# The second batch's Fourier transform in a fused FFT, SoLU and maxout kernel: x loaded earlier, its items set to other places

## The chip, the cores and the metric

The kernel runs on one core of a Trainium2 chip. The metric is the device time of one execution in microseconds (us), the lower the better. The kernel before took 2872.8 us (median of three runs, 2868.82 to 2873.03).

## The reference

Three layers one after the other, on x of 8 batches x 3072 positions x 256 channels:

```
X = rfft(x, axis=1);  y = irfft(X * (filt_r + 1j * filt_i), n=3072)          # per batch and channel
h = y @ w_in                                    # 256 -> 1024
solu = h * softmax(h);  ln = (solu - mean) / sqrt(var + 1e-6) * g_ln
z = ln @ w_out                                  # 1024 -> 256
m = maximum(maximum(z @ w1, z @ w2), z @ w3)    # 256 -> 768
out = m @ w_out2                                # 768 -> 256, float32
```

## The kernel before, in words

Engines are named as in the profile: PE (TensorE), PEld (its weight load), DVE (VectorE), ACT (ScalarE), POOL (GpSimd), SP (SyncE, which only issues transfers). Each works through its own queue in order. A framework schedules: it takes the program in the order in which it is written, moves instructions of one engine past each other by times that it reckons itself, and puts in the waits. What stands in each queue is therefore fixed before the kernel runs.

**Precision.** Values are kept as two 16-bit halves, a high and a low one, so nearly every product is three matmuls (high x high, high x low, low x high), and every result that PE makes is read twice: ACT writes the high half, DVE or POOL the difference.

**The steady loop.** A batch is cut into 6 groups of 512 positions (NG = 6), 48 groups in all. A group's work on PE is a string of items, whose order is the string ORDER (L27; the first group has FIRST, L26): z (two halves, `z_item`, 48 matmuls), h (four of 128 positions, `h_item`, 12 matmuls each, always for the next group or the one after), m (six blocks of the maxout, `m_item`, 18 matmuls each, whose three results lie in three PSUM buffers until ACT L573 and DVE L575 have taken their maximum), o (two, `o_item`, 36 each) and d (`d_item`, the last step of the inverse FFT for the group after next). PSUM has six small buffers ("r") for all of these but h, which has one of its own. `s0` to `s4` in the string are places: what the planner at L838 to L895 has put there (`put(batch, group, place, function, ...)`) is run at this point.

**The FFT of the next batch** goes into these places. Its steps for batch b: `load_x` (six pieces of 512 KB, POOL L106, into the one buffer called "x"), `absmax` (DVE L111, one per piece), `x_spread` and `x_scale` (the largest value over all partitions, through one PE product called amps, then small DVE operations), `prep_a` (ACT L153 and DVE L154 split a piece into halves xh, xl), `do_a` (six items "a", 6 matmuls each, results to DRAM scr_a by SP L176), `load_b` (POOL L184, reads bin back from scr_a and needs all six written), `do_b` (eight items "b"; their products with the filter on DVE L219/L220 and POOL L227/L228, then `late`: two halves yhl, transposed by SP L264 into yt), `do_c` (eight items "c" on yt, results over SP L388/L395 to scr_z), `load_d` and d. For batches 2 to 7 these are spread over nearly two batches' groups. For batch 1 there are only the first batch's groups 0 to 4: b stands in groups 2 and 3, c from the end of group 2 to group 4.

**What differs for batch 1 before the change.** Its x is loaded when the last setup job of group 0 has been put in the program (L1148 to L1150). Its filter table ft is multiplied by a factor on ACT when it has come (`scale_f`, L211), and yhl is split by ACT L257 and POOL L258; for later batches the factor is in the split itself (ACT L260, DVE L261).

**Setup.** The first batch's FFT is done ahead of the loop in float32. Its last step turns zx (which lies in buffer "x") by PE L354 (`first_turn_z`). The weights are converted and scaled meanwhile; of w_out2 the last piece is fetched at L1084, and its float32 form is put into the buffer "x" as wst (L1085), when zx has been read, by the jobs that group 0 runs at its `x0` places (`last`, `colsum`, `scale`, `split`, L1090 to L1102). The second halves of the maxout weights wm are written by POOL L704 just ahead of group 0. The second batch's x takes buffer "x" after wst, the third batch's after the second's, when the last `prep_a` has read it.

## Time and profile before

| | |
|---|---|
| median of three runs | 2872.8 us |
| the profiled execution: its time, its span | 2866.93 us, 2865.1 us |
| PE busy | 2801.6 us, 98% of the span |
| DVE, ACT, POOL busy | 70%, 43%, 40% |
| granted TensorE clock, mean | 0.990 |
| DMA | 352.73 MB, 123 GB/s on the mean |

The table is read so: PE is busy for 98% of the span, and its clock is nearly always granted in full. What is not PE's work is 63.5 us of idle time, and some time at the lower clock. The profile's slices of the span put nearly all of it into the first seventh, before 425 us: the setup, and groups 0 to 4 of the first batch.

### The profile page before, as it was taken

To read this page: it belongs to the slowest core of one execution; us is meant where nothing else is said; L and a number is where in the kernel's file an instruction comes from. 1 tells how busy PE (TensorE), PEld (TensorE's weight loads), DVE (VectorE), ACT (ScalarE), POOL (GpSimd) and SP (SyncE) were. 2 spreads that over 40 slices of the span, in tenths; PEclk is the share of its full clock that TensorE was granted. 3 is DMA by queue.
4 is the path that set the end of the run, shared out by engine and by line. 5 is a ranking of instruction groups with operands and counts; after the bars stand their busy time and mean duration, and the time that the engine had idled before them with its cause. 6 is when DMAs were issued, how large, how long until landed. Compare 5 with 4: busy or idle time off the path is not lost.

```text
span 2865.1 us, 49331 instructions
## 1 busy us (share of the span) xinstructions
PE 2801.6 (98%) x18923; PEld 1567.6 (55%) x18924; DVE 2000.6 (70%) x4158; ACT 1237.0 (43%) x2024; POOL 1138.6 (40%) x1208
## 2 busy tenths in 40 slices
PE   8799989999999999999999999999999999999999
PEld 7544545555555555555555555555555555555555
DVE  6787658777776776777677777777777677666563
ACT  5644444444443444444453444444444344333332
POOL 5343543444334443344334433344442444323222
PEclk8899999999999999999999999999999999999999
DMA  8445885668456874578555875567844576422221
GB/s 252 104 111 158 143 171 156 115 138 142 110 148 120 142 130 107 155 133 138 106 133 137 145 126 116 152 119 137 140 110 107 118 152 104 101 56 61 58 47 28
DMA packets 718380, 352.73 MB, mean 123 GB/s; under 512 B 620544, under 2 KB 663936, under 8 KB 718144
## 3 DMA queue, kind: packets, MB, share of 16 engines
q1 hardware_dynamic: 689040, 242.57, 44.0%
q0 software_dynamic: 28960, 106.95, 14.5%
q8 instruction: 148, 2.42, 0.4%
q14 instruction: 88, 0.72, 0.1%
q10 hardware_dynamic: 144, 0.07, 0.0%
HBM read 126.13 MB, written 71.30 MB: 69 GB/s over the span
## 4 chain that ended last, share of the span: by engine, by line
PE 90%; DMA 3%; POOL 2%; DVE 2%; issue 2%; ACT 1%; SPq 0%; ACTq 0%; POOLq 0%; DVEq 0%
PE mps L567 12%; PE mps L569 12%; PE mps L568 12%; PE hps L461 6%; PE hps L462 6%; PE hps L463 5%; PE zps L547 5%; PE zps L550 5%; PE zps L548 5%; PE ops L596 4%; PE ops L595 4%; PE ops L594 4%; DMA ft<-in_filt_dram 1%; PE bps L242 1%; PE bps L243 1%
## 5 line engine op out<-in xcount | busy, mean ns | idle before, releaser
L508 POOL TENSOR_TENSOR ul<-u,uh 128x1024 f16<-128x1024 f32 x191 | 410.7, 2150 | 1097.8 <-ACT uh L507 942.7
L567 PE MATMUL mps<-z,wm 128*128 128x512 f16 x1728 | 654.9, 379 | 2.6 <-DVE z L537 1.9
L569 PE MATMUL mps<-z,wm 128*128 128x512 f16 x1728 | 654.7, 379 | 1.1 <-DVE z L537 1.1
L568 PE MATMUL mps<-z,wm 128*128 128x512 f16 x1728 | 654.9, 379 | 0.0
L575 DVE SCALAR_TENSOR_TENSOR am<-mps,am 128x512 f32<-128x512 f32 x576 | 395.1, 686 | 211.2 <-PE mps L569 129.0
L472 DVE TENSOR_REDUCE mx<-hps 128x1 f32<-128x1024 f32 (+1 forms) x194 | 234.6, 1209 | 225.8 <-PE hps L463 225.5
L478 ACT ACTIVATE u<-hps,mx,scl 128x1024 f32<-128x1024 f32 (+1 forms) x194 | 231.6, 1194 | 311.2 <-DVE mx L475 307.1
L578 ACT ACTIVATE h<-am 128x512 f16<-128x512 f32 x288 | 180.5, 627 | 406.6 <-DVE am L575 406.6
L579 POOL TENSOR_TENSOR h<-am,h 128x512 f16<-128x512 f32 x240 | 278.1, 1159 | 188.5 <-ACT h L578 185.7
L596 PE MATMUL ops<-wo,h 128*128 128x256 f16 x1152 | 314.8, 273 | 4.0 <-DVE h L579 4.0
L594 PE MATMUL ops<-wo,h 128*128 128x256 f16 x1152 | 314.8, 273 | 0.5 <-ACT o L600 0.4
L595 PE MATMUL ops<-wo,h 128*128 128x256 f16 x1152 | 314.7, 273 | 0.0
L461 PE MATMUL hps<-win,y 128*128 128x512 f16 x768 | 293.9, 383 | 8.7 <-ACT y L436 6.5
L462 PE MATMUL hps<-win,y 128*128 128x512 f16 x768 | 293.5, 382 | 0.0
L463 PE MATMUL hps<-win,y 128*128 128x512 f16 x768 | 292.8, 381 | 0.0
L547 PE MATMUL zps<-ln,wo 128*128 128x512 f16 x752 | 285.4, 380 | 0.5 <-ACT o L600 0.5
L548 PE MATMUL zps<-ln,wo 128*128 128x512 f16 x752 | 285.4, 380 | 0.0
L489 DVE SCALAR_TENSOR_TENSOR u<-hps,mx,u 128x1024 f32<-128x1024 f32 (+1 forms) x194 | 246.4, 1271 | 51.5 <-ACT u L478 48.8
L507 ACT ACTIVATE uh<-u 128x1024 f16<-128x1024 f32 x192 | 202.7, 1056 | 184.1 <-DVE u L489 180.3
L569 PEld LDWEIGHTS <-wm 128*128 128x128 f16 x1728 | 169.0, 98 | 205.0 <-issue 1.3
L568 PEld LDWEIGHTS <-wm 128*128 128x128 f16 x1728 | 169.0, 98 | 201.7 <-issue 4.3
L567 PEld LDWEIGHTS <-wm 128*128 128x128 f16 x1728 | 169.0, 98 | 198.4
(232 smaller groups left out, 4482.4 us busy)
## 6 DMA issues: line engine op xcount, KB each, us to landing
out_dram<-o SPq DMA_DIRECT2D x95, 256.0 KB, 2.3
ft<-in_filt_dram POOLq DMA_DIRECT2D x56, 384.0 KB, 5.5
xt<-in_x_dram POOLq DMA_DIRECT2D x42, 512.0 KB, 8.2
scr_a<-ao SPq DMA_DIRECT2D x42, 512.0 KB, 3.3
bin<-scr_a POOLq DMA_DIRECT2D x56, 384.0 KB, 6.2
scr_z<-zt SPq DMA_DIRECT2D x56, 384.0 KB, 3.0
din<-scr_z POOLq DMA_DIRECT2D x42, 512.0 KB, 5.0
bt<-in_dft_b_dram POOLq DMA_DIRECT2D x56, 144.0 KB, 3.0
```

Source lines behind the costliest of these rows:

```text
L461: PE.matmul(o, y[:, dc, 0, tk], win[:, 0, dc, w], start=(dc == 0), stop=False)
L462: PE.matmul(o, y[:, dc, 0, tk], win[:, 1, dc, w], start=False, stop=False)
L463: PE.matmul(o, y[:, dc, 1, tk], win[:, 0, dc, w], start=False, stop=(dc == 1))
L508: (V if (b, g, i) == (0, 0, 3) else G).tensor_tensor(ul, u, uh, op=ALU.subtract)
L547: PE.matmul(ps, wo1[:, 0, c, w], ln[:, 0, c], start=(c == 0), stop=False)
L548: PE.matmul(ps, wo1[:, 1, c, w], ln[:, 0, c], start=False, stop=False)
L567: PE.matmul(pss[k], wm[k][:, 0, dc, w], z[:, dc, 0], start=(dc == 0), stop=False)
L568: PE.matmul(pss[k], wm[k][:, 1, dc, w], z[:, dc, 0], start=False, stop=False)
L569: PE.matmul(pss[k], wm[k][:, 0, dc, w], z[:, dc, 1], start=False, stop=(dc == 1))
L594: PE.matmul(o, h2[:, j, 0, tk], wo2[:, 0, j], start=(j == 0), stop=False)
L595: PE.matmul(o, h2[:, j, 0, tk], wo2[:, 1, j], start=False, stop=False)
L596: PE.matmul(o, h2[:, j, 1, tk], wo2[:, 0, j], start=False, stop=(j == 5))
```

## The change

1. Two more places per group, `s5` behind x1 and `s6` behind m4.
2. The second batch's x is loaded right behind the first batch's last turn: the six `load_x(1, i)` stand ahead of `pads()`, and buffer "x" no longer holds wst. For this w_out2's float32 form is made in place, in the three buffers that its pieces were fetched into (`last` with the new `low`), and its column sums and its split go in three parts instead of two and one.
3. The second batch's `absmax`, `x_spread`, `x_scale` and first `prep_a` go to group 0, its six a items over group 1 (one each place instead of two), its b and c items into groups 2 and 3 alternately, the last c to the first place of group 4 instead of the second.
4. The third batch's x is loaded piece by piece in groups 1 to 3 instead of six pieces in a row; its loads, and its first two `prep_a` on ACT, keep the program's order in their queues.
5. `scale_f` is gone. The second batch's yhl is split as the later ones' are: ACT with the factor, and DVE in POOL's stead.

```
@@ -24,7 +24,7 @@
 
 
 FIRST = "h0 m0 x0 h1 m1 x0 x0 h2 m2 x0 x0 x0 s0 s1 s2 x2 h3 m3 d m4 m5 g0 f o0 s3 o2 g1 s4"
-ORDER = "z0 s0 z1 s1 h2 m0 x0 x0 x1 m1 x0 x0 m2 s2 x2 h3 m3 d m4 m5 g0 f o0 s3 o2 g1 s4"
+ORDER = "z0 s0 z1 s1 h2 m0 x0 x0 x1 s5 m1 x0 x0 m2 s2 x2 h3 m3 d m4 s6 m5 g0 f o0 s3 o2 g1 s4"
 
 
 @with_exitstack
@@ -103,7 +103,9 @@
             x_t[b] = one.tile([128, 6144], F32, tag="x", name="xt")
         src = x[b].rearrange("(p r) d -> p (r d)", r=24)
         c = slice(i * 1024, (i + 1) * 1024)
-        G.dma_start(out=x_t[b][:, c], in_=src[:, c])
+        ins = G.dma_start(out=x_t[b][:, c], in_=src[:, c])
+        if b == 2:
+            tc.keep_in_program_order(ins)
 
     def absmax(b, i):
         if i == 0:
@@ -150,7 +152,9 @@
         xh = two.tile([128, 1024], F16, tag="zo", name="xh")
         xl = two.tile([128, 1024], F16, tag="bin", name="xl")
         src = x_t[b][:, s * 1024:(s + 1) * 1024]
-        S.activation(xh, src, AF.Copy, scale=scl[b][:, 0:1])
+        ins = S.activation(xh, src, AF.Copy, scale=scl[b][:, 0:1])
+        if b == 2 and s < 2:
+            tc.keep_in_program_order(ins)
         V.scalar_tensor_tensor(xl, src, scl[b][:, 0:1], xh, op0=ALU.mult, op1=ALU.subtract)
         xhl[b, s] = (xh, xl)
 
@@ -206,9 +210,6 @@
         bt_t[0, u], ct_t[0, u] = t[:, 0:4], t[:, 4:8]
 
     yT_t, zt_t = {}, []
-
-    def scale_f(b, u):
-        S.activation(f_t[b, u], f_t[b, u], AF.Copy, scale=pf[:, 1:2])
 
     def products(pss, ft, u, outs=None):
         yfs = []
@@ -253,14 +254,10 @@
             for dc in range(2):
                 yv = yfs[dc].rearrange("p k r s -> p k (r s)")
                 yhl = yhl_t[2 * (u % 2) + dc]
-                if b < 2:
-                    S.activation(yhl[:, :, 0:48], yv, AF.Copy)
-                    G.tensor_tensor(yhl[:, :, 48:96], yv, yhl[:, :, 0:48], op=ALU.subtract)
-                else:
-                    S.activation(yhl[:, :, 0:48], yv, AF.Copy, scale=pf[:, 1:2])
-                    V.scalar_tensor_tensor(
-                        yhl[:, :, 48:96], yv, pf[:, 1:2], yhl[:, :, 0:48], op0=ALU.mult, op1=ALU.subtract
-                    )
+                S.activation(yhl[:, :, 0:48], yv, AF.Copy, scale=pf[:, 1:2])
+                V.scalar_tensor_tensor(
+                    yhl[:, :, 48:96], yv, pf[:, 1:2], yhl[:, :, 0:48], op0=ALU.mult, op1=ALU.subtract
+                )
                 SP.dma_start_transpose(out=yt[:, dc], in_=yhl.rearrange("p k s -> p (k s)"))
         return early, late
 
@@ -640,9 +637,12 @@
                     wprep(v, (raw[:, k:k + 1], True))
                 return
             S.activation(dst, raw.bitcast(F32).rearrange("p a (n w) -> p a n w", w=2)[:, :, :, 1], AF.Copy, scale=REBIAS)
-            lo = raw.rearrange("p a (n w) -> p a n w", w=2)[:, :, :, 0]
-            top = raw.bitcast(U16).rearrange("p a (n w) -> p a n w", w=4)[:, :, :, 1]
-            G.tensor_scalar(lo, top, TOP, 7.5 * 2.0 ** -8 - 0.5, op0=ALU.mult, op1=ALU.add)
+            low(raw)
+
+    def low(raw):
+        lo = raw.rearrange("p a (n w) -> p a n w", w=2)[:, :, :, 0]
+        top = raw.bitcast(U16).rearrange("p a (n w) -> p a n w", w=4)[:, :, :, 1]
+        G.tensor_scalar(lo, top, TOP, 7.5 * 2.0 ** -8 - 0.5, op0=ALU.mult, op1=ALU.add)
 
     def wconv(pairs):
 
@@ -668,7 +668,7 @@
         av = []
 
         def sizes():
-            for v, (pool, tag) in zip(parts, ((one, "o"), (two, second))):
+            for v, (pool, tag) in zip(parts, ((one, "o"), (two, second), (two, second))):
                 kn = v.shape[1]
                 ab = pool.tile([128, 1024], F16, tag=tag, name="wab").bitcast(BF16)[:, :kn * n]
                 av.append(ab.rearrange("p (k n) -> p k n", k=kn))
@@ -812,11 +812,7 @@
         held[0] = None
 
     def do_b(b, u):
-        if u == 0 and b == 1:
-            scale_f(b, 0)
         run(b_item(b, u))
-        if u < 7 and b == 1:
-            scale_f(b, u + 1)
         if u < 6:
             load_tabs(b, u + 2)
             load_b(b, u + 2)
@@ -836,7 +832,7 @@
         run(it)
 
     NT = NB * NG
-    slots = [[[] for _ in range(5)] for _ in range(NT)]
+    slots = [[[] for _ in range(7)] for _ in range(NT)]
 
     def put(b, c, s, f, *a):
         if b >= 0:
@@ -846,13 +842,13 @@
 
         if b == 1:
             for i in range(6):
-                put(0, i // 4, (3, 4, 0)[i // 2], absmax, 1, i)
-            put(0, 1, 0, x_spread, 1)
-            put(0, 1, 1, x_scale, 1)
-            put(0, 1, 1, prep_a, 1, 0)
-            put(0, 1, 1, prep_a, 1, 1)
+                put(0, 0, (1, 2, 3)[i // 2], absmax, 1, i)
+            put(0, 0, 3, x_spread, 1)
+            put(0, 0, 4, x_scale, 1)
+            put(0, 0, 4, prep_a, 1, 0)
+            put(0, 1, 0, prep_a, 1, 1)
             for s in range(6):
-                put(0, 1, 2 + s // 2, do_a, 1, s)
+                put(0, 1, (0, 1, 5, 2, 6, 3)[s], do_a, 1, s)
             for u in range(2):
                 put(0, 1, 2 * u, load_tabs, 1, u)
                 put(0, 1, 4, load_b, 1, u)
@@ -877,15 +873,15 @@
             put(b - 2, 5, 0, load_c, b, 0)
         if b + 1 < NB:
             at = (
-                ((0, 1, 3), (0, 1, 4), (0, 2, 0), (0, 2, 1), (0, 2, 2), (0, 2, 3)) if b == 1 else
+                ((0, 1, 4), (0, 2, 1), (0, 2, 3), (0, 3, 0), (0, 3, 5), (0, 3, 3)) if b == 1 else
                 [(b - 1, *s) for s in ((0, 0), (0, 2), (0, 4), (1, 1), (1, 3), (2, 0))]
             )
             for i in range(6):
                 put(*at[i], load_x, b + 1, i)
 
         if b == 1:
-            at = [(2, 1), (2, 2), (2, 3), (2, 4), (3, 1), (3, 2), (3, 3), (3, 4)]
-            ct = [(2, 3), (2, 4), (3, 1), (3, 2), (3, 3), (3, 4), (4, 0), (4, 1)]
+            at = [(2, 1), (2, 5), (2, 2), (2, 6), (2, 4), (3, 5), (3, 2), (3, 6)]
+            ct = [(2, 2), (2, 6), (2, 3), (3, 0), (3, 2), (3, 6), (3, 3), (4, 0)]
         else:
             at = [(u // 2, 2 * (u % 2)) for u in range(8)]
             ct = [((u + 1) // 2, (4, 1)[u % 2]) for u in range(8)]
@@ -1082,15 +1078,26 @@
     first_turn_z(4)
     first_turn_z(5)
     get(19)()
-    wo2_32 = wview(one.tile([128, 6144], F32, tag="x", name="wst"), 6, 256)
-    todo += blocks(w_out2, wo2_32)
+    for i in range(6):
+        load_x(1, i)
     pads()
     G.dma_start(out=dA, in_=dft_a[:, 0:2])
 
+    wo2_32 = []
+
     def last():
         for i in range(17, 20):
-            pre(i)()
-        conv(17, 18, 19)()
+            pair = got.pop(i)[0].rearrange("p a (n w) -> p a n w", w=2)
+            low(pair.rearrange("p a n w -> p a (n w)"))
+            wo2_32.append(pair[:, :, :, 1].bitcast(F32))
+            lo, hi = pair[:, :, :, 0], pair[:, :, :, 1]
+            V.scalar_tensor_tensor(lo, hi, -0x80000000, lo, op0=ALU.bitwise_and, op1=ALU.bitwise_or)
+            S.activation(wo2_32[-1], wo2_32[-1], AF.Copy, scale=REBIAS)
+            V.scalar_tensor_tensor(hi, hi, 3, lo, op0=ALU.logical_shift_left, op1=ALU.bitwise_or)
+
+    def split_o2():
+        for i, v in enumerate(wo2_32):
+            wsplit(wo2[:, :, 2 * i:2 * i + 2], v, pw["o2"], G)
 
     def set_kap():
         V.tensor_tensor(kap, pw["o1"][:, 0:1], pw["m"][:, 0:1], op=ALU.mult)
@@ -1098,8 +1105,8 @@
         V.tensor_scalar(kap, kap, 2.0 ** -14, None, op0=ALU.mult)
 
     jobs.append(last)
-    jobs += colsum([wo2_32[:, 0:4], wo2_32[:, 4:6]], 256, wmax, 12, "zo")
-    jobs += [scale("o2", 12, 1), split(wo2, wo2_32, "o2", G), set_kap]
+    jobs += colsum(wo2_32, 256, wmax, 12, "zo")
+    jobs += [scale("o2", 12, 1), split_o2, set_kap]
 
     for t in range(NT):
         b, c = divmod(t, NG)
@@ -1145,9 +1152,6 @@
             elif k == "x":
                 if i == 0:
                     fill(1)
-                    if not jobs and NB > 1 and 1 not in x_t and t == 0:
-                        for k in range(6):
-                            load_x(1, k)
                 if i == 1 and nx2 and nx2[1] == 0:
                     flush()
                     load_d(*nx2)
```

How the queues move, at three places on POOL and ACT. Line numbers behind "in the kernel after" are those of the changed file, in which L496 is what L499 was, L403 was L406, L505 was L508, L576 was L579, L188 was L184, L193 was L189, L475 was L478, L570 was L573, L504 was L507, L575 was L578; L257 is its `late`.

POOL just ahead of group 0 in the kernel before (din is a load for the first batch's d items, wm the maxout weights' low halves, st a small power):

```order
L645 TENSOR_SCALAR wraw<-wraw 128x512
L406 DMA din_2003<-scr_94 128x1024
L499 TENSOR_TENSOR st<-st,mhalf 128x4
L704 TENSOR_TENSOR wm_79<-w_880,wm_79 128x384
L704 TENSOR_TENSOR wm_79<-w_881,wm_79 128x384
L704 TENSOR_TENSOR wm_78<-wln,wm_78 128x2x384
```

and in the kernel after:

```order
L645 TENSOR_SCALAR wraw<-wraw 128x512
L403 DMA din_2033<-scr_94 128x1024
L496 TENSOR_TENSOR st<-st,mhalf 128x4
L106 DMA xt<-in_x_dram 128x1024
L704 TENSOR_TENSOR wm_79<-w_880,wm_79 128x384
L704 TENSOR_TENSOR wm_79<-w_881,wm_79 128x384
L106 DMA xt<-in_x_dram 128x1024
L704 TENSOR_TENSOR wm_78<-wln,wm_78 128x2x384
L106 DMA xt<-in_x_dram 128x1024
```

The second batch's first piece of x now stands ahead of the weights' low halves; the fourth to sixth follow between and behind their second halves, and none is left where all six stood, behind the split of w_out2 in group 0.

POOL around the first loads of bin, the second batch's way back from scr_a, in the kernel before (xt here is the third batch's x):

```order
L508 TENSOR_TENSOR ul<-u,uh 128x1024
L106 DMA xt<-in_x_dram 128x1024 x6
L184 DMA bin<-scr_a_93 96x8x256
L508 TENSOR_TENSOR ul<-u,uh 128x1024
L184 DMA bin<-scr_a_93 96x8x256
L189 DMA bt<-in_dft_b_dram 96x768
```

and in the kernel after:

```order
L106 DMA xt<-in_x_dram 128x1024
L496 TENSOR_TENSOR st<-st,mhalf 128x4
L581 TENSOR_SCALAR st<-st,kap 128x4
L576 TENSOR_TENSOR h_2164<-am,h_2164 128x512
L505 TENSOR_TENSOR ul<-u,uh 128x1024
L188 DMA bin<-scr_a_93 96x8x256 x2
L106 DMA xt<-in_x_dram 128x1024
L505 TENSOR_TENSOR ul<-u,uh 128x1024
L193 DMA bt<-in_dft_b_dram 96x768
```

Two pieces of the third x are now ahead of the bin loads, one right behind them, and three stand much later, in groups 2 and 3.

ACT in group 3, in the kernel before (u is an h item's exponential, am the first step of an m item's maximum, ft the filter table, uh the high half of u, h that of the maximum):

```order
L478 ACTIVATE u,st<-hps,mx,scl 128x1024
L573 ACTIVATE am<-mps 128x512
L211 ACTIVATE ft<-ft,pf 128x768
L507 ACTIVATE uh<-u 128x1024
L573 ACTIVATE am<-mps 128x512
L578 ACTIVATE h_3618<-am 128x512 x2
```

and in the kernel after:

```order
L475 ACTIVATE u,st<-hps,mx,scl 128x1024
L570 ACTIVATE am<-mps 128x512
L504 ACTIVATE uh<-u 128x1024
L575 ACTIVATE h_3661<-am 128x512
L570 ACTIVATE am<-mps 128x512
L257 ACTIVATE yhl_90<-p_3731,pf 128x8x48
L257 ACTIVATE yhl_91<-p_3737,pf 128x8x48
```

The filter's own pass no longer stands between the first and the second am; the split of yhl, with the factor pf, follows the second.

## Rows read from the trace of the kernel before

**Rows 1.** The page's first part: busy time, share, instructions of each engine.

```profile
PE 2801.6 (98%) x18923; PEld 1567.6 (55%) x18924; DVE 2000.6 (70%) x4158; ACT 1237.0 (43%) x2024; POOL 1138.6 (40%) x1208
```

**Rows 2.** Windows by stage: length, then busy by engine, clock, DMA share, GB/s.

```profile
138.90:198.08 59.18, 51.80 (x276) 27.72 (x274) 49.07 (x103) 31.98 (x50) 28.86 (x26) 0.97 0.52 119
...
259.75:327.31 67.56, 61.07 (x486) 34.57 (x485) 48.72 (x95) 26.09 (x44) 35.61 (x47) 0.95 0.69 161
327.31:403.03 75.72, 63.34 (x554) 36.86 (x551) 43.50 (x94) 29.76 (x52) 40.26 (x52) 0.93 0.97 166
403.03:423.53 20.50, 16.61 (x126) 8.62 (x126) 10.33 (x32) 7.99 (x15) 9.21 (x13) 0.92 1.09 231
423.53:2865.10 2441.57, 2437.24 (x16319) 1331.50 (x16317) 1703.13 (x3525) 1031.13 (x1684) 941.52 (x963) 1.00 0.58 117
```

**Rows 3.** Windows at the lower clock behind 138 us: the longest, all four summed.

```profile
360.40:370.60 10.20, 5.06 (x70) 3.46 (x70) 4.12 (x9) 5.50 (x9) 5.36 (x5) 0.50 1.11 171
...
sum 23.90, PE 16.71 PEld 10.41 DVE 12.49 ACT 8.10 POOL 12.06; mean PE 4.18 PEld 2.60 DVE 3.12 ACT 2.02 POOL 3.02
```

**Rows 4.** Waits of PE: us in total, times, the longest.

```profile
PE cps L377 <- ACT am L573: 8.4, 1, 8.4
PE bps L242 <- DMA bin<-scr_a: 6.5, 1, 6.5
PE ops L596 <- DVE h L579: 4.0, 1, 4.0
PE cps L377 <- DMA yt<-yhl: 3.9, 2, 3.2
```

**Rows 5.** Timeline of DVE: start, us, instruction, count, idle before and its releaser.

```profile
146.42 1.27 DVE L489 SCALAR_TENSOR_TENSOR u<-hps,mx,u 128x1024 f32<-128x1024 f32 x1
...
186.83 1.22 DVE L111 TENSOR_REDUCE xm<-xt 128x1 f32<-128x1024 f32 x1 [3.09 <-DMA xt<-in_x_dram]
187.97 0.68 DVE L579 TENSOR_TENSOR h<-am,h 128x512 f16<-128x512 f32 x1
...
208.86 0.29 DVE L129 TENSOR_REDUCE amr<-amps 128x1 f32<-128x128 f32 x1 [3.84 <-PE amps L127]
...
212.59 2.47 DVE L154 SCALAR_TENSOR_TENSOR xl<-xt,scl,xh 128x1024 f16<-128x1024 f32 x2
```

**Rows 6.** Timeline of POOL: x's loads, bin's first, the maxout weights' low halves.

```profile
134.53 1.79 POOL L704 TENSOR_TENSOR wm<-w,wm 128x384 f16<-128x384 f32 x2 [0.40 <-ACT wm L703]
137.33 1.75 POOL L704 TENSOR_TENSOR wm<-wln,wm 128x768 f16<-128x768 f32 x1 [1.01 <-ACT wm L703]
...
175.49 3.26 POOL L106 DMA_DIRECT2D xt<-in_x_dram  x6
...
254.97 3.24 POOL L106 DMA_DIRECT2D xt<-in_x_dram  x6 [3.18 <-DVE xl L154]
272.67 0.83 POOL L184 DMA_DIRECT2D bin<-scr_a  x1 [14.46 <-DMA scr_a<-ao]
```

**Rows 7.** Timeline of ACT: the filter's pass in group 3.

```profile
361.98 0.94 ACT L211 ACTIVATE ft<-ft,pf 128x768 f32<-128x768 f32 x1 [10.85 <-DMA ft<-in_filt_dram]
```

**Rows 8.** The chain, by time: start, us, what (a matmul's pace, the filter's way).

```profile
201.70 1.73 PE zps L550 x8
...
348.84 13.05 DMA ft<-in_filt_dram
```

**Rows 9.** Line L354, zx's turns: ns min/median/max, first and last start (us).

```profile
L354 PE MATMUL zps<-eye_f,zx x48: 272/273/421, 79.1 to 138.8; 128*128 128x128 f32 x48
```

**Rows 10.** Tile xt, all of the span: its loads.

```profile
DMA to landing us min/median/max: 4.1/8.2/13.8
```

**Rows 11.** Tile yt between 270 and 430 us: its transposes.

```profile
DMA to landing us min/median/max: 3.1/4.6/13.8
```

**Rows 12.** Line L261 from 425 to 2000 us: ns min/median/max; DVE's idle before it.

```profile
L261 DVE SCALAR_TENSOR_TENSOR yhl<-p,pf,yhl x72: 602/620/1102, 536.9 to 1975.3; 128x384 f16<-128x384 f32 x72
...
  ACT yhl L260: 82.0, 54
```

More of the change, by code (lines that the diff above doesn't have):

```diff
@@ L642, in wprep, with low @@
             S.activation(dst, raw.bitcast(F32).rearrange("p a (n w) -> p a n w", w=2)[:, :, :, 1], AF.Copy, scale=REBIAS)
-            lo = raw.rearrange("p a (n w) -> p a n w", w=2)[:, :, :, 0]
-            top = raw.bitcast(U16).rearrange("p a (n w) -> p a n w", w=4)[:, :, :, 1]
-            G.tensor_scalar(lo, top, TOP, 7.5 * 2.0 ** -8 - 0.5, op0=ALU.mult, op1=ALU.add)
+            low(raw)
+    def low(raw):
+        lo = raw.rearrange("p a (n w) -> p a n w", w=2)[:, :, :, 0]
+        top = raw.bitcast(U16).rearrange("p a (n w) -> p a n w", w=4)[:, :, :, 1]
+        G.tensor_scalar(lo, top, TOP, 7.5 * 2.0 ** -8 - 0.5, op0=ALU.mult, op1=ALU.add)
     def wconv(pairs):
@@ L670, in sizes @@
         def sizes():
-            for v, (pool, tag) in zip(parts, ((one, "o"), (two, second))):
+            for v, (pool, tag) in zip(parts, ((one, "o"), (two, second), (two, second))):
                 kn = v.shape[1]
@@ L838 @@
     NT = NB * NG
-    slots = [[[] for _ in range(5)] for _ in range(NT)]
+    slots = [[[] for _ in range(7)] for _ in range(NT)]
     def put(b, c, s, f, *a):
@@ L1084, with split_o2 @@
     get(19)()
-    wo2_32 = wview(one.tile([128, 6144], F32, tag="x", name="wst"), 6, 256)
-    todo += blocks(w_out2, wo2_32)
+    for i in range(6):
+        load_x(1, i)
     pads()
     G.dma_start(out=dA, in_=dft_a[:, 0:2])
+    wo2_32 = []
     def last():
         for i in range(17, 20):
-            pre(i)()
-        conv(17, 18, 19)()
+            pair = got.pop(i)[0].rearrange("p a (n w) -> p a n w", w=2)
+            low(pair.rearrange("p a n w -> p a (n w)"))
+            wo2_32.append(pair[:, :, :, 1].bitcast(F32))
+            lo, hi = pair[:, :, :, 0], pair[:, :, :, 1]
+            V.scalar_tensor_tensor(lo, hi, -0x80000000, lo, op0=ALU.bitwise_and, op1=ALU.bitwise_or)
+            S.activation(wo2_32[-1], wo2_32[-1], AF.Copy, scale=REBIAS)
+            V.scalar_tensor_tensor(hi, hi, 3, lo, op0=ALU.logical_shift_left, op1=ALU.bitwise_or)
+    def split_o2():
+        for i, v in enumerate(wo2_32):
+            wsplit(wo2[:, :, 2 * i:2 * i + 2], v, pw["o2"], G)
     def set_kap():
@@ L1100 @@
     jobs.append(last)
[L1101 to L1102 removed]
+    jobs += colsum(wo2_32, 256, wmax, 12, "zo")
+    jobs += [scale("o2", 12, 1), split_o2, set_kap]
     for t in range(NT):
@@ L1147 @@
                     fill(1)
-                    if not jobs and NB > 1 and 1 not in x_t and t == 0:
-                        for k in range(6):
-                            load_x(1, k)
                 if i == 1 and nx2 and nx2[1] == 0:
```

48 lines of the change are left out of this document (20 added, 28 removed).

## The prediction

> **What bounds the kernel now.** I read the busy line first: PE works for 2801.6 of 2865.1 us [rows 1], so only PE's waits, or time at the lower clock, can be won. The windows by stage say where these are [rows 2]. From 423.53 us to the end PE is busy for 2437.24 of 2441.57 us at a granted clock of 1.00. What each queue holds from the middle of group 4 on is the same in both kernels, so whatever is won or lost before that point is carried to the end one for one. In groups 0, 2, 3 and the start of group 4 PE idles for 7.38, 6.49, 12.38 and 3.89 us. (z0 of group 1 starts at 198.08, of group 2 at 259.75, of group 3 at 327.31, of group 4 at 403.03.)
>
> The list of PE's waits names what ended them [rows 4]: 4.0 us for h of DVE L579 (group 0), 6.5 for bin (group 2), 8.4 for an am of ACT L573 (group 3), 3.9 for yt (group 4). One step further back, on the timelines: h was late because the x maximum ahead of it on DVE stood 3.09 us for x's landing [rows 5]; bin was late because POOL issued it at 272.67, after scr_a had come back, behind the six pieces of the third x issued from 254.97 on [rows 6]; am was late because ACT stood 10.85 us in L211 for the filter [rows 7], whose way took 13.05 us [rows 8].
>
> The granted clock is the last view. Behind each of these waits stands a stretch at 0.50, the lower of the two levels (1.2 of 2.4 GHz): four windows of 23.90 us with 16.71 us of PE work [rows 3]. At full clock this work takes half, so 8.36 us are lost to it.
>
> **What the change takes away.** Group 0: the maxima of x stand early in the group instead of ahead of h: 4.0; the other 3.4 us of its idle time I leave where they are. Group 2: the bin wait, since only two single pieces of x stand ahead of bin and the a items end half a group sooner: 6.49. Group 3: L211 is gone, and what it held with it: 12.38. Group 4: yt is filled earlier, by b items that end in group 3: 3.89. Clock, if the waits ahead of it go: 8.36. Sum 35.1 us.
>
> **What the change adds.** For each: both ends, and the value I take.
>
> 1. POOL now stands at x's first piece until zx's last turn has read the buffer, 138.8 + 0.27 = 139.1 [rows 9]; in before POOL did the low halves of wm from 134.53 on [rows 6]. A load holds POOL for 3.26 / 6 = 0.54. So the last low half is ready at 139.1 + 0.54 + 1.79 + 0.54 + 1.75 = 143.7, 4.6 us later than before. PE begins at 138.90 with h0's 12 matmuls of 0.216 us (1.73 / 8, [rows 8]), to 141.5, and has m0's products of the high halves next. Ends 0 and 2.2; taken 0.5.
> 2. Three of the x maxima stand on DVE ahead of the first u (L489, at 146.42 in before, [rows 5]); behind it are the am that free m's PSUM, and h1 needs the buffer that u reads. The third piece is issued at 143.7. With the shortest way of x's loads, 4.1 us [rows 10], it is there at 147.8; maximum 1.22, u 1.27 and four small steps of some 0.2 bring u's end to 151.1. PE has m0 and m1 to do ahead of h1: 36 matmuls, 7.8 us, to 149.3. So 1.8 us are lost by the shortest way and 5.9 by the median, 8.2. The pieces are issued 2.3 us apart now and not in a row, so I lean to the shortest, and part of the loss falls into the 3.4 us of idle time that I left. Ends 0 and 5.9; taken 1.5.
> 3. The first a item, now at group 1's first place, needs the chain from amr (208.86) to the first xl (212.59 plus half of 2.47): 5.0 us [rows 5]. Ahead of it PE has z0, 24 matmuls, 5.2 us. Ends 0 and 2.5 (if another xl stands ahead); taken 0.6.
> 4. c0 stands behind 66 matmuls and a b item's start after b0, some 15 us, in which b0's products, its split and the transpose must pass; the transpose alone takes 3.1 to 13.8 us [rows 11]. Ends 0 and the 3.9 of the yt waits in before; taken 1.
> 5. Six maxima of the third x stand singly in groups 1 to 3, five of them soon behind their loads. Ends 0 and five times 3.09 [rows 5], 15.5; taken 2, since most loads have over half a group.
> 6. The 16 subtractions of yhl move from POOL to DVE, at 0.62 us each, and DVE waits for ACT's half ahead of them: 82.0 / 54 = 1.52 us a time in the later batches [rows 12]. In groups 2 and 3 DVE has 48.72 + 43.50 = 92.2 us of work beside PE's 61.07 + 63.34 = 124.4 [rows 2]. 16 x 0.62 makes it 102.1, and with 16 x 1.52 = 24.3 of waits 126.5: 2.1 above PE. Ends 0 and 24.3; taken 3, the 2.1 and a little for unevenness.
>
> At nothing I cost w_out2 in place: its parts go through as many passes on ACT and DVE as before (three of each kind), and in before its split was done when the x loads were issued behind it at 175.49 [rows 6], 12.5 us before DVE began the h that o waited for, at 187.97 [rows 5]. Only what overruns these 12.5 us would cost time.
>
> The costs add to 8.6 us and the net gain is 35.1 - 8.6 = 26.5. The profiled execution took 2866.93 us (span 2865.1), so it becomes 2840.4. It stands 5.9 below the median of three, 2872.8; against that median the forecast is 2846.3, and I put down 2846.
>
> For items 2 and 5 the way of a 512 KB load is the open figure, and the trace has 4.1, 8.2 and 13.8 us [rows 10]. The Trainium skill, "DMA: Bandwidth & Descriptors", section "Anatomy of one DMA — SWDGE (gpsimd) path", gives about 2.0 us and the bytes at 436 GB/s; by that an estimate is 3.2 us, and both items would cost under 1 us. No load of x in this trace was that quick, so the measured way decides.
>
> **The rivals.**
>
> A. DVE becomes the bound of groups 2 and 3. Items 5 and 6 then cost not 5 but some 20 of their 39.8 us (8 and 12). For it: 126.5 beside 124.4 us. Against it: DVE's other waits are for PE, and shrink when PE is not held up. The gain is 35.1 - 3.6 - 20 = 11.5: 2861.
>
> B. The moved subtractions are slow beside POOL. L261 has a median of 620 and a longest of 1102 ns [rows 12]: 16 x 0.48 = 7.7 us more on DVE, which in groups 2 and 3 has no room left. 2846 + 7.7 = 2854. Against it: the median of 72 is within 18 ns of the least. The Trainium skill, "SBUF — State Buffer", section "Who interferes with whom", has the rule for this: DVE and GpSimd share one pair of ports, and the one that comes second waits for the other's whole instruction. By that the subtraction, with both its inputs in SBUF, would stand behind POOL's passes; the trace's median says that this is rare.
>
> C. The filter and yt come late all the same. L219 on DVE reads the filter itself now, so the 13.05 us way [rows 8] can hold DVE where it held ACT. Then group 3's 12.38 and the clock behind it, 2.5 (half of 5.06, [rows 3]), stay: 2846 + 14.9 = 2861. For it: the DMA share in that stage is already 0.97 [rows 2]. Against: ACT passes all m items, DVE's queue reaches L219 only when PE has done the b item, which gives the filter longer.
>
> D. Slower. The eight maxima that stand close behind their loads (three of item 2, five of item 5) meet ways of 13.8 instead of 8.2 us: 8 x 5.6 = 45 us of DVE standing still, in which h, am and z stand too. From the point where all losses pass 35.1 us, it is slower; with 34 of the 45 reaching PE and the 5.1 of items 1, 3, 4 and 6 it is 2872.8 + 4 + 2 of lower clock behind the new waits: 2879. Against it: 13.8 is the longest of all loads, and single loads press the queues less than six in a row.
>
> E. The waits only change their names: each stage is then held by the next chain (b's way to c, say) at the same length. 2872. Against it: groups 2 and 3 each wait once and long, for one instruction.
>
> **How the numbers follow.** Forecast 0.64, its own range 2837 to 2854; A 0.15, B 0.07, C 0.08, D 0.04, E 0.02. The range of 8 in 10 reaches down to where nearly nothing of the added costs arrives (35.1 less 1: 2838.7, and 4 us for what of group 0's left idle time goes too: 2835), and up past A and C to 2863. About 0.2% (5.7 us) is what a measurement of this kernel can tell from no change. Faster than that are the forecast, B, and nearly all of A and C: 0.91; within 0.2% are E and a tail of A and C: 0.05; slower is D: 0.04.
>
> **What would show it.** Right: z0 of group 1 starts near 193 us, of group 2 near 255, of group 3 near 316, of group 4 near 378; no wait of DVE for x next to the h of o in group 0; no wait of PE for bin and none for am behind a filter; no window at half clock behind 150 us. New and small: PE's waits at m0 and h1 in group 0 (items 1 and 2), at the first a item, for yt at c0, DVE's waits for x in groups 1 to 3 and for yhl in groups 2 and 3; their sum on PE should be near 8.6. Wrong: DVE busy or waiting for the whole of groups 2 and 3 with PE waiting for z, h or am (A); L261's counterpart near 1 us (B); DVE waiting for ft (C); clock still 0.93 to 0.95 there, which would leave the 8.36 unwon.

## The result and the profile after

The kernel after takes 2840.2 us (median of 4) where the kernel before takes 2870.8 in the same runs: ratio of the means 0.9897, interval 0.9867 to 0.9927. A second measurement of the unchanged pair gave 2847.1 against 2862.2, ratio 0.9949, interval 0.9930 to 0.9969. Both are faster; 2846 was forecast, between 2835 and 2863. The profiled execution took 2841.28 us (span 2839.5), 25.6 less than that of before.

The busy line, as in [rows 1]:

```profile
PE 2795.4 (98%) x18923; PEld 1563.6 (55%) x18924; DVE 2015.1 (71%) x4174; ACT 1233.8 (43%) x2021; POOL 1125.8 (40%) x1194
```

Windows by stage, as in [rows 2] (length, then busy by engine, clock, DMA share, GB/s). The bounds are the starts of h0 of group 0 and of z0 of groups 1 to 5, and the end. First the kernel after:

```profile
138.53:193.69 55.16, 51.57 (x278) 27.67 (x276) 50.99 (x103) 35.34 (x57) 33.65 (x30) 0.97 0.52 131
193.69:255.35 61.66, 61.60 (x330) 32.37 (x328) 50.49 (x97) 32.43 (x50) 18.91 (x14) 1.00 0.45 120
255.35:320.80 65.45, 61.45 (x549) 35.45 (x548) 48.15 (x100) 25.86 (x44) 36.97 (x52) 1.00 0.95 182
320.80:383.81 63.01, 61.08 (x523) 35.50 (x519) 50.02 (x103) 27.55 (x48) 33.81 (x44) 0.97 1.05 200
383.81:440.75 56.94, 56.94 (x348) 30.63 (x347) 41.60 (x88) 25.95 (x42) 17.93 (x15) 1.00 0.55 132
440.75:2839.50 2398.75, 2394.36 (x16067) 1307.80 (x16065) 1670.72 (x3465) 1011.45 (x1652) 925.90 (x950) 1.00 0.57 117
```

and the last two stages of the kernel before, cut at the same items:

```profile
403.03:466.40 63.37, 59.48 (x378) 32.27 (x378) 42.63 (x92) 28.22 (x47) 24.80 (x26) 0.97 0.68 160
466.40:2865.10 2398.70, 2394.37 (x16067) 1307.85 (x16065) 1670.84 (x3465) 1010.91 (x1652) 925.92 (x950) 1.00 0.58 117
```

From z0 of group 5 on the two are alike to 0.05 us. So everything was won in the stretch from h0 of group 0 to z0 of group 5: 327.50 us before, 302.22 after, 25.28 less. Groups 0 and 1 together give 4.03 of it (120.85 to 116.82), groups 2 to 4 give 21.25. By the windows, 20.6 us of it are PE's idle time (30.1 to 9.6) and 4.7 are work that no longer runs at the lower clock. What PE waited for in the stretch, as in [rows 4] (us in total, times, the longest):

```profile
PE mps L565 <- DVE wm L707: 2.8, 1, 2.8
PE bps L243 <- ACT am L570: 2.1, 2, 1.8
PE cps L374 <- DVE y L434: 1.7, 1, 1.7
PE mps L564 <- ACT am L570: 1.2, 1, 1.2
PE ops L593 <- POOL h L576: 0.6, 1, 0.6
```

None of the four long waits is left. Two windows at the lower clock remain, one behind the first of these waits and one behind the third; [rows 3] had four of 23.90 us:

```profile
144.75:148.20 3.45, 3.45 (x9) 1.31 (x10) 3.45 (x6) 3.18 (x6) 3.43 (x4) 0.53 0.69 180
363.40:366.90 3.50, 3.44 (x52) 2.46 (x52) 3.24 (x8) 1.68 (x4) 3.33 (x5) 0.51 0.88 204
```

The 2.8 us are new. They end with DVE's pass on wm, which took 1.02 us in the kernel before, begun when the first two of POOL's passes of [rows 6] had ended (timeline of DVE: start, us, instruction, idle before):

```profile
136.55 1.02 DVE L707 SCALAR_TENSOR_TENSOR wm<-wln,pwm,wm 128x768 f16<-128x768 f32 x1 [3.56 <-ACT wm L706]
```

and 4.41 in the kernel after (DVE, then POOL):

```profile
140.28 4.41 DVE L707 SCALAR_TENSOR_TENSOR wm<-wln,pwm,wm 128x768 f16<-128x768 f32 x1 [2.79 <-ACT wm L706]
148.90 1.00 DVE L707 SCALAR_TENSOR_TENSOR wm<-wln,pwm,wm 128x768 f16<-128x768 f32 x1
```

```profile
139.00 0.60 POOL L106 DMA_DIRECT2D xt<-in_x_dram  x1 [4.64 <-PE zps L351]
139.62 1.79 POOL L704 TENSOR_TENSOR wm<-w,wm 128x384 f16<-128x384 f32 x2
141.35 0.56 POOL L106 DMA_DIRECT2D xt<-in_x_dram  x1
141.93 1.65 POOL L704 TENSOR_TENSOR wm<-wln,wm 128x768 f16<-128x768 f32 x1
143.51 0.57 POOL L106 DMA_DIRECT2D xt<-in_x_dram  x1
144.10 2.23 POOL L704 TENSOR_TENSOR wm<-w,wm 128x384 f16<-128x384 f32 x2
```

DVE's pass starts in the middle of POOL's passes on wm and ends 1.1 us behind the third of them, and the fourth and fifth take 2.23 instead of 1.79: each engine held up the other. Of DVE's and ACT's waits in the stretch these matter below:

```profile
DVE xm L113 <- DMA xt<-in_x_dram: 16.9, 5, 5.4
DVE yhl L258 <- ACT yhl L257: 12.2, 11, 2.6
```

```profile
ACT yhl L257 <- POOL p L229: 23.1, 14, 4.0
ACT yhl L257 <- POOL p L231: 7.0, 2, 6.3
```

### The profile page after: what moved, and what is told of

The parts are those of the page before. It is cut to its first block, busy times and chain, and to the rows that moved or that the text cites. A ratio compares the mean times of both kernels' runs of the same rounds, so it can differ in the third digit from the quotient of the medians.

```text
span 2839.5 us, 49318 instructions
## 1 busy us (share of the span) xinstructions
PE 2795.4 (98%) x18923; PEld 1563.6 (55%) x18924; DVE 2015.1 (71%) x4174; ACT 1233.8 (43%) x2021; POOL 1125.8 (40%) x1194
## 4 chain that ended last, share of the span: by engine, by line
PE 91%; DVE 3%; POOL 2%; issue 1%; DMA 1%; ACT 1%; SPq 0%; ACTq 0%; POOLq 0%; DVEq 0%
PE mps L564 12%; PE mps L566 12%; PE mps L565 12%; PE zps L544 6%; PE zps L545 6%; PE zps L547 6%; PE hps L458 5%; PE hps L459 5%; PE hps L460 5%; PE ops L593 4%; PE ops L592 4%; PE ops L591 4%; PE cps L374 1%; PE cps L375 1%; PE bps L244 1%
## 5 line engine op out<-in xcount | busy, mean ns | idle before, releaser
L505 POOL TENSOR_TENSOR ul<-u,uh 128x1024 f16<-128x1024 f32 x191 | 410.8, 2151 | 1101.0 <-ACT uh L504 946.5
L475 ACT ACTIVATE u<-hps,mx,scl 128x1024 f32<-128x1024 f32 (+1 forms) x194 | 231.7, 1195 | 327.0 <-DVE mx L472 312.3
L575 ACT ACTIVATE h<-am 128x512 f16<-128x512 f32 x288 | 180.4, 626 | 393.6 <-DVE am L572 393.6
L576 POOL TENSOR_TENSOR h<-am,h 128x512 f16<-128x512 f32 x240 | 279.4, 1164 | 175.4 <-ACT h L575 172.6
L504 ACT ACTIVATE uh<-u 128x1024 f16<-128x1024 f32 x192 | 202.8, 1056 | 185.0 <-DVE u L486 181.2
```

The source lines that it names most:

```text
L505: (V if (b, g, i) == (0, 0, 3) else G).tensor_tensor(ul, u, uh, op=ALU.subtract)
```

## The experiments

Each row of this table is one profiled execution, cut at the items named above (the start of the first h matmul and of the first z matmul of a group, read from the trace): the first column is where h0 of group 0 starts, that is the length of the setup.

| kernel | h0 at | groups 0, 1 | group 2 | group 3 | group 4 | stretch | rest |
|---|---|---|---|---|---|---|---|
| before | 138.90 | 120.85 | 67.56 | 75.72 | 63.37 | 327.50 | 2395.0 |
| before again | 138.76 | 119.85 | 67.95 | 73.42 | 68.88 | 330.10 | 2395.0 |
| part 5 alone | 137.36 | 119.78 | 67.61 | 60.15 | 67.63 | 315.17 | 2395.0 |
| part 4 alone | 135.33 | 120.04 | 67.54 | 83.73 | 68.61 | 339.92 | 2395.3 |
| parts 1 to 3 | 137.98 | 116.74 | 70.36 | 64.42 | 57.04 | 308.56 | 2395.4 |
| parts 1 to 4 | 131.29 | 116.17 | 70.69 | 66.73 | 56.94 | 310.53 | 2395.4 |
| after without part 4 | 134.35 | 116.18 | 63.28 | 63.16 | 56.96 | 299.58 | 2395.0 |
| after | 138.53 | 116.82 | 65.45 | 63.01 | 56.94 | 302.22 | 2395.0 |
| after again | 138.16 | 116.54 | 66.38 | 68.54 | 56.93 | 308.39 | 2395.1 |
| after, third | 133.45 | 116.94 | 66.16 | 62.51 | 57.20 | 302.81 | 2395.1 |
| after, x behind wm | 135.81 | 117.12 | 65.99 | 62.35 | 58.34 | 303.80 | 2395.0 |
| after, wm on DVE | 136.32 | 112.99 | 65.79 | 62.24 | 58.54 | 299.56 | 2395.1 |
| after, products on DVE | 136.85 | 116.57 | 63.73 | 63.19 | 56.97 | 300.46 | 2395.1 |
| joined | 138.92 | 112.87 | 61.36 | 59.70 | 56.93 | 290.86 | 2395.1 |

(The parts' numbers are those of the section on the change. Where b and c items stand differs between the kernels, so groups 2 to 4 are best compared as a sum.) The setup differs by up to 7.6 us between the rows, and by 5.1 between three executions of the kernel after. Times of whole runs carry this; the stretch does not. But the stretch differs too between executions of one kernel: by 2.6 us for the kernel before and by 6.2 for the kernel after, mostly in groups 2 to 4. Most kernels below have one profile, so a difference of a few us in groups 2 to 4 is not shown by it alone.

**Part 5 alone.** The kernel before, with scale_f and its calls gone and late split as in the diff's hunk:

```
-        if u < 7 and b == 1:
-            scale_f(b, u + 1)
...
-                    G.tensor_tensor(yhl[:, :, 48:96], yv, yhl[:, :, 0:48], op=ALU.subtract)
...
+                S.activation(yhl[:, :, 0:48], yv, AF.Copy, scale=pf[:, 1:2])
+                V.scalar_tensor_tensor(
```

> The kernel before with part 5 alone: no pass over the filter on ACT (L211), yhl of the second batch split by ACT with the factor and DVE in POOL's stead. Theory (the terms of the prediction): group 3's wait of 8.4 us for am and what followed it goes, so group 3 loses not 12.4 but 1 to 4 us, and the lower clock behind it (2.5) goes too; in all 9 to 13 us faster, ratio 0.9955 to 0.9969, with no new long wait of PE. Rival (the filter's transfer is late, not its pass): DVE L219 waits about 10 us for ft where ACT waited, PE waits the same 8 us for am, ratio 0.999 to 1.001.

2853.1 against 2861.8, ratio 0.9971 (0.9953 to 0.9989); stretch 12.33 shorter, 11.26 of it in groups 2 to 4. Group 3 has no idle time and no lower clock now:

```profile
324.75:384.90 60.15, 60.15 (x555) 35.37 (x551) 49.85 (x104) 27.84 (x48) 33.82 (x44) 1.00 0.96 205
```

while bin and yt (of the PE waits) stay:

```profile
PE cps L370 <- DMA yt<-yhl: 6.8, 3, 5.2
PE bps L239 <- DMA bin<-scr_a: 6.3, 1, 6.3
```

The pass was the cost in group 3. Whether part of what it gives comes back as yt waits in group 4 these profiles do not tell: group 4 is 4.3 us longer than in the first profile of before and 1.3 shorter than in the second.

**Part 4 alone.** The kernel before, with the third x's pieces at the new places and in program order:

```
-                ((0, 1, 3), (0, 1, 4), (0, 2, 0), (0, 2, 1), (0, 2, 2), (0, 2, 3)) if b == 1 else
+                ((0, 1, 4), (0, 2, 1), (0, 2, 3), (0, 3, 0), (0, 3, 5), (0, 3, 3)) if b == 1 else
+        if b == 2:
+            tc.keep_in_program_order(ins)
```

> The kernel before with part 4 alone: the third batch's x loaded singly over groups 1 to 3 and not six in a row ahead of bin. Theory (the six loads made scr_a and bin late): the wait of 6.5 us for bin in group 2 falls below 2 us and the lower clock behind it goes, 7 to 10 us faster, ratio 0.9965 to 0.9976; scr_a's landing near its median of 3 us instead of 14. Rival (the a items end too late, the loads are no part of it): bin is issued within 2 us of where it was relative to the last a item, PE waits 5 us or more, ratio 0.999 to 1.001.

2872.0 against 2861.8, ratio 1.0028 (1.0009 to 1.0048), and the stretch 12.42 longer. Neither theory had it slower. Of PE's waits:

```profile
PE cps L381 <- DMA yt<-yhl: 12.3, 4, 4.8
PE bps L246 <- DMA bin<-scr_a: 6.7, 1, 6.7
PE cps L381 <- ACT am L577: 4.7, 1, 4.7
```

The bin wait is the same to 0.2 us with two pieces of x ahead of bin as with six, and POOL stands 13.2 us for the last scr_a (14.5 in before):

```profile
264.92 0.83 POOL L188 DMA_DIRECT2D bin<-scr_a  x1 [13.16 <-DMA scr_a<-ao]
```

Yet the loads were not without effect. The last two writes of scr_a took 3.7 and 3.5 us to land here, and 7.2 and 5.8 in before, beside the six loads. So POOL issued bin 9.55 us after z0 of group 2 began, and not 12.92. Then bin took 7.6 us to land instead of 4.0, and PE waited as long as before. Why bin's way grew is not shown. What the a items do is the same in both: the last of them ends 0.2 us after z0 of group 2 begins.

The added time is in group 3 (83.73 beside 75.72 and 73.42 in the two profiles of before; group 4 is as long as in the second of these). There DVE and ACT wait for transfers (over the stretch):

```profile
DVE xm L113 <- DMA xt<-in_x_dram: 25.9, 7, 5.8
```

```profile
ACT ft L215 <- DMA ft<-in_filt_dram: 24.8, 5, 9.3
```

In before the wait for x is 9.7 and the one for ft 22.9, so of these two only the first has grown much; and PE's yt waits are 12.3 us where the two profiles of before have 3.9 and 5.0.

**Parts 1 to 3, and parts 1 to 4.** The kernel after with parts 4 and 5 undone, or part 5 alone undone (the hunks above, backwards).

> The kernel after without parts 4 and 5: x of the second batch early, a, b and c items at the new places, the third x in a row, the filter's pass on ACT and the split on POOL as before. Theory (the terms add): group 0's 4.0 and group 4's 3.9 with their clock are won (11 us), 3 to 5 are lost again at m0 of group 0, the waits for am behind the filter's pass (8.4) stays; 5 to 9 us faster, ratio 0.9969 to 0.9983. Rival (the earlier places of b alone loosen the filter and bin as well): no PE wait above 3 us in groups 2 and 3, 18 to 25 us faster, ratio 0.9913 to 0.9937.

> The kernel after with part 5 undone: the filter's pass on ACT and POOL's split of yhl are back. Theory (the pass is what cost 12.4 us): PE waits 6 to 10 us for an am behind L211 again; 8 to 13 us slower than the kernel after, ratio to before 0.9932 to 0.9950. Rival (with the b items spread singly the filter is early enough, and part 5 is worth nothing or costs DVE time): within 2 us of the kernel after, ratio 0.9890 to 0.9905.

Parts 1 to 3: 2844.8, 0.9930 (0.9910 to 0.9950); parts 1 to 4: 2846.0, 0.9942 (0.9919 to 0.9966). Parts 1 to 3 have a stretch 18.94 shorter, the rival's 18 to 25. Their waits in groups 2 to 4:

```profile
PE cps L377 <- DVE y L437: 6.1, 2, 4.4
PE mps L567 <- ACT am L573: 2.8, 2, 1.9
PE bps L242 <- ACT am L573: 1.3, 1, 1.3
```

No wait for bin, with part 4 undone, and none for yt: the earlier places did it. The last a item ends 6.4 us before z0 of group 2 begins, and the six loads, which move up with the a items, were all issued by 235.59, 16 us ahead of the last write of scr_a, which took 3.4 us. One wait of 4.4 us contradicts the rival's "none above 3". The wait of 8.4 us for am is gone too, with the filter's pass still there: the largest for am is 1.9. With part 4 added the stretch is 1.97 longer. Part 5 makes 8.3 us on top of parts 1 to 4 (310.53 to 302.22), the low end of what was expected, but 2.1 and 7.7 by the other two profiles of the kernel after, and 9.0 on top of parts 1 to 3. The waits of 6 to 10 us for am that were expected without it did not come, so what it gives there comes in small pieces.

**The kernel after without part 4.**

> The kernel after with part 4 undone: the third x's six pieces in a row again, at the end of group 1 and in group 2. The stretch is from the start of h0 of group 0 to the start of z0 of group 5: 327.5 us in the kernel before, 302.2 in the kernel after. Theory (the bin wait came from a items that ended too late, and part 4 only moves loads into the filter's and bin's traffic): 298 to 302.5, no wait of PE for bin, the time within 3 us of the kernel after or better. Rival (the prediction's step: the loads in a row hold up scr_a and bin): PE waits 3 us or more for bin or yt, stretch 306 to 312, ratio to before 0.991 or more.

2835.2 against 2863.7, ratio 0.9902 (0.9878 to 0.9925), not to be told from the kernel after by time; stretch 299.58, of which groups 2 to 4 are 183.40 against 185.40. DVE's wait for x falls from 16.9 to 0.9 us, and there is no wait for bin. By groups 2 to 4 the loads spread singly cost 2.0 us of PE with part 5 and 2.5 without it. Both are smaller than what executions of one kernel differ by, so this cost is likely and not shown.

In this execution DVE's pass on wm took 1.02 us, though POOL was held at x's first piece as before. PE's last product of the setup ran at full clock here, and at 0.62 in the kernel after (the windows of these 48 matmuls, first the kernel after, then this one):

```profile
133.68:138.05 4.37, 4.37 (x49) 4.37 (x49) 0.69 (x1) 1.89 (x4) 0.68 (x1) 0.62 0.44 146
```

```profile
131.12:133.96 2.84, 2.84 (x50) 2.83 (x50) 0.34 (x1) 0.96 (x2) 0.62 (x1) 1.00 0.62 216
```

POOL, whose first load waits for zx's last turn right behind this product, was therefore free earlier, and DVE came as POOL's first passes ended:

```profile
135.44 1.79 POOL L700 TENSOR_TENSOR wm<-w,wm 128x384 f16<-128x384 f32 x2
137.18 0.56 POOL L106 DMA_DIRECT2D xt<-in_x_dram  x1
137.90 1.73 POOL L700 TENSOR_TENSOR wm<-wln,wm 128x768 f16<-128x768 f32 x1 [0.17 <-ACT wm L699]
```

```profile
137.11 1.02 DVE L703 SCALAR_TENSOR_TENSOR wm<-wln,pwm,wm 128x768 f16<-128x768 f32 x1 [2.79 <-ACT wm L702]
```

**x's loads behind wm, and wm on DVE alone.** Two ways to keep POOL's passes off DVE's:

```
-        if b == 2:
+        if b <= 2:                      # x behind wm
             tc.keep_in_program_order(ins)
```

```
-        eng = (V, G, G)[k]
+        eng = (V, V, V)[k]              # wm on DVE
```

> The kernel after, with the second batch's six loads kept in program order on POOL, so behind all low halves of wm. Theory (POOL, held at x's first piece, moves its passes on wm onto DVE's own pass on wm, which then takes 4.41 us instead of 1.02): L707's first instance back at 1.0 to 1.5 us, the gap of 2.81 us ahead of m0 falls to about 1, no half clock there; stretch from h0 to z0 of group 5 298 to 300, 3 to 4 us faster than the kernel after. Rival (what PE waits for there is ready late for another reason, ACT's passes): the gap stays at 2 us or more, 302 to 303. A third outcome, x landing later than the maxima stand: new DVE waits ahead of h1, 303 to 306.

> The kernel after, with all low halves of wm made on DVE and none on POOL, x's loads held as before at the last turn. Theory (DVE's pass was slowed by POOL's passes beside it, not by the loads): the L707 passes of 768 columns take 1.0 to 1.1 us each though POOL issues x's loads at the same time; gap ahead of m0 below 1.5 us. Rival (the loads' issue on POOL, or the traffic, slows DVE): one of these passes takes 2 us or more.

Behind wm: DVE's pass is back at 1.02 us, and the gap at m0 at 0.34 and 0.78. This proves less than was meant: the last setup product ran at full clock in this execution (2.84 us), and with that the pass took 1.02 without this edit too. And the stretch is 303.80: the third outcome. The maxima of x's last pieces stand in the end of group 0 again, PE waits 1.1 us for ACT's h and 0.5 for POOL's there, and groups 0 and 1 gain nothing (117.12). Time 2842.9, 0.9929 (0.9908 to 0.9950). On DVE alone, with all six of x's loads issued by POOL between 136.78 and 139.99:

```profile
L707 DVE SCALAR_TENSOR_TENSOR wm<-w,pwm,wm x4: 609/612/615, 135.3 to 139.5; 128x384 f16<-128x384 f32 x4
L707 DVE SCALAR_TENSOR_TENSOR wm<-wln,pwm,wm x4: 1005/1016/1467, 136.6 to 141.5; 128x768 f16<-128x768 f32 x4
```

Three of the four wide passes take 1.0 us, two of them beside the loads, though the last setup product ran at 0.62 of the clock here. The slowest, 1.47, began with a pass of POOL's on wraw (140.06, 0.67 us) and ended 0.80 us behind it: POOL's passes slowed DVE, not its loads. Groups 0 and 1 gain 3.83 us; groups 2 to 4 give 1.17 of it back. Time 0.9923 (0.9893 to 0.9953).

**The second half of the filter products on DVE.**

```
-            G.tensor_tensor(pr[:, :, 0, :], p1[:, :, 0, :], p2[:, :, 1, :], op=ALU.subtract)
-            G.tensor_tensor(pr[:, :, 1, :], p1[:, :, 1, :], p2[:, :, 0, :], op=ALU.add)
+            eng.tensor_tensor(pr[:, :, 0, :], p1[:, :, 0, :], p2[:, :, 1, :], op=ALU.subtract)
+            eng.tensor_tensor(pr[:, :, 1, :], p1[:, :, 1, :], p2[:, :, 0, :], op=ALU.add)
...
+            yfs.extend(products(pss, ft, u, eng=V if b == 1 else G))
```

> The kernel after, with the second half of the second batch's filter products (L228 and L229) on DVE instead of POOL. Theory (what is left of PE's waits in group 2, 1.2 and 2.1 us for am, comes from ACT standing in L257 for POOL's product with am behind it): ACT's wait there falls from 23 us to under 12, these waits of PE go, stretch 298.5 to 300.5. Rival (DVE has no room for 32 more passes of about 0.35 us): PE waits for z, h or am of DVE instead, stretch 302 to 308.

Half of the theory. Groups 2 to 4 are 1.51 us shorter, less than executions of one kernel differ by, the waits for am at b items fall from 2.1 to 0.8, and DVE has room. But ACT's wait in L257 does not fall below 12 us, it is 20.4 for DVE's product now; the wait of 1.2 for am stays. Time 2834.8, 0.9903 (0.9882 to 0.9923).

**Joined, beside the kernel after.** Part 4 undone, wm on DVE, the products on DVE; and the kernel after unchanged in the same call.

> The kernel after with three edits together: part 4 undone, the low halves of wm all on DVE, the second half of the second batch's filter products on DVE. The stretch from h0 of group 0 to z0 of group 5 was 302.2 us in the kernel after; alone the edits gave 299.6 (part 4 undone), 299.6 (wm on DVE: 3.8 won in groups 0 and 1, 1.2 lost behind) and 300.5 (products on DVE). Theory (they act at different places and add): 294 to 296.5, ratio to before 0.987 to 0.990, 4 to 8 us faster than the kernel after in the same call. Rival (DVE, with both moves, becomes the bound of groups 2 and 3, and the wins overlap): 298 to 301, not told from the kernel after.

> The kernel after, unchanged, on the same chip and in the same call as the joined one. The stretch is the same order of queues as in its first profile: 302.2 us, within 2 us. Theory (what differs between executions of one kernel lies in the setup ahead of h0, where PE runs the first batch's last products at either level of the clock): h0 starts between 131 and 139 us, and where it starts early, the pass of DVE on wm meets fewer passes of POOL and the gap at m0 is shorter. Rival: the gap of 2.8 us at m0 is there in each execution.

Joined: 2828.5 (median of 6) against 2862.2 of before, ratio 0.9882 (0.9856 to 0.9908); the kernel after on the same chip 2847.1, 0.9949 (0.9930 to 0.9969), the runs of the two not overlapping (highest 2834.4, lowest 2844.0). That is 18.7 us, where 4 to 8 were expected. Its stretch of 290.86 is below the expected range, and 11.4 shorter than the shortest of the kernel after's three, where the parts alone make 7.1; with one profile of each, the excess is not explained. PE waits for about 2 us in all; the two longest lines are:

```profile
PE hps L454 <- DVE u L482: 1.0, 2, 0.6
PE cps L370 <- DVE y L430: 0.4, 1, 0.4
```

No lower clock is left in it either. The kernel after's second profile has a wait that the first had not, in group 3, and so a stretch of 308.39, not within 2 us of 302.2 as expected:

```profile
PE cps L374 <- DMA yt<-yhl: 6.6, 1, 6.6
```

**Before once more, after once more.** Both unchanged, for the spread between executions.

> The kernel before, unchanged, once more with a profile. It asks how much the stretch from h0 of group 0 to z0 of group 5 differs between executions of one kernel: 327.5 us in the first profile of before, 302.2 and 308.4 in two of the kernel after (the second with a wait of 6.6 us for yt that the first has not). Theory (the transfers' ways differ between executions, the work does not): 321 to 334, with the four long waits (am, bin, h, yt) there again, each other by up to a few us, and 2395.0 us from z0 of group 5 to the end as in every profile so far. Rival (before's four waits are one execution's bad luck): the stretch is 315 or less.

> The kernel after, unchanged, a third profile on the chip that runs the kernel before in the same call. Theory (the transfers' ways differ between executions): stretch 301 to 309, a yt wait of 0 to 7 us, the gap of 2.5 to 2.8 us at m0 there again. Rival (the yt wait of 6.6 us is what the kernel mostly has, the first profile was the lucky one): 307 to 310 with that wait of 5 us or more at the same c item.

Before: 330.10, with its four long waits again:

```profile
PE bps L242 <- DMA bin<-scr_a: 6.5, 1, 6.5
PE cps L377 <- ACT am L573: 5.4, 1, 5.4
PE cps L377 <- DMA yt<-yhl: 5.0, 2, 2.7
PE ops L596 <- DVE h L579: 3.1, 1, 3.1
```

After: 302.81, with 2.7 us of yt in three waits, the longest 1.8. Its h0 starts early, at 133.45, and yet the pass on wm takes 4.41 us: not an early h0 shortens it, as was expected for the second profile, but a last setup product at full clock (it ran at 0.62 here too). In the seven profiles in which POOL stands at x's first piece and has passes on wm, the 48 matmuls took 2.84 us in two (parts 1 to 4, after without part 4), with a pass of 1.02, and 4.1 to 4.5 in five, with a pass of 4.41.

## Why the prediction came out right, and where it did not

**Carried one for one: shown.** From z0 of group 5 to the last matmul there are 2395.0 to 2395.4 us in all fourteen profiles.

**The sum: 26.5 forecast, 25.3 in the pair of first profiles** (two profiles of before and three of after make 19.1 to 27.9). That the first pair comes so close is in part luck. PE's idle time fell to 9.6 us, where the forecast left 12.0 (8.6 of costs and the 3.4 of group 0); the clock gave 4.7 where 8.36 stood in the sum; the two misses nearly cancel. So do the signs: z0 of groups 3 and 4 came 4.8 and 5.8 us later than the 316 and 378 put down, and group 4 made up for it. The four waits went as forecast, but not all for the reason given.

- *Group 0, 4.0.* Right: no wait for h behind a maximum of x. That groups 0 and 1 are just 4.03 us shorter is chance: of the 3.4 us of idle time that were left alone all but 0.8 went too, and the new 2.8 came (7.38 to 3.59 in all).
- *Group 3, 12.38.* Right: part 5 alone took 15.6 us from group 3, 12.3 from the stretch. But parts 1 to 3, with the pass still there, took the wait of 8.4 us away as well, so in the whole change the term has two causes, each enough for that wait. Rival C is out: DVE has no wait for ft in the trace of after.
- *Group 2, 6.49: the step that failed.* "Bin was late because POOL issued it ... behind the six pieces of the third x" took for the cause what was a part of it. POOL did not wait for its own loads, it waited 14.46 us for scr_a [rows 6]. The loads made the last writes of scr_a slower (7.2 and 5.8 us beside 3.7 and 3.5), but part 4 alone, which took them away and had bin issued 3.4 us earlier, left PE's wait at 6.7. Parts 1 to 3, in which the last a item ends 6.5 us earlier and the loads with it, removed it. The forecast had named the a items as well, so the term came out though its first reason was not enough.
- *Group 4, 3.89.* It went: PE has no idle time in group 4 in the first profile. But yt is waited for in group 3 in the other two (item 4).
- *Clock, 8.36.* Two windows of 6.89 us of PE's work remain, one of them at 363.40, where the forecast wanted none behind 150 us, so about 3.4 were not won.
- *Items 1 and 2, 2.0 together.* The size was 2.8 and the clock behind it, the mechanism another one. No maximum of x waited in group 0, and POOL's halves were not what PE waited for: DVE's own third of wm was, held up by POOL's passes that the held load had pushed onto it.
- *Item 3, 0.6.* Group 1 has 0.06 us of idle time: nothing.
- *Item 4, 1, ends 0 and 3.9.* Three profiles have 0, 6.6 and 2.7 us of yt waits: the upper end was too low.
- *Item 5, 2.* DVE waits for 16.9 us, above the upper end of 15.5, and nearly all of it is hidden: the kernels without part 4 are 2.0 and 2.5 us shorter. The size fits, but executions of one kernel differ by more.
- *Item 6, 3, by DVE's 126.5 us.* The size is right (3.3 in PE's waits for am), the way is not: DVE's waits are 12.2 us, half of those taken from the later batches. What held PE is more likely ACT, standing for POOL's product in front of yhl with am queued behind it: with the products on DVE the waits for am at b items fell from 2.1 to 0.8, though ACT still stood for 20.4 us there and the 1.2 stayed.

Rival A did not come: DVE is busy for 98.2 us in groups 2 and 3, and PE has 122.5. Nor did B: the 16 subtractions have a median of 620 ns and a longest of 829. The rule weighed there (the Trainium skill, "SBUF — State Buffer", section "Who interferes with whom") did decide something in this change, at another place than where I looked for it: DVE's passes on wm. In seven profiles such a pass began during a single pass of POOL's, and it ended 0.80 to 0.82 us behind that one, which agrees. The 4.41 us agree only in part: by that rule DVE waits for the pass that POOL is in, by an estimate 0.2 us from 140.28 (139.62 and half of 1.79), and it came in behind the third.

What stays open. Why part 4 alone costs 10 to 12 us: that the waits for x and yt are longer with it is shown, that the spread loads make yt later is only argued. Why bin's way grew with part 4 alone is open too, and why DVE's pass on wm lost to three passes of POOL's. Why one execution of the kernel after has a yt wait of 6.6 us and others have 0 to 2.7 is not known, nor how often it has. And the second measurement's smaller gain (15 us against 31) is of the size that such a wait and the setup's length can make, which is no proof.
